# A causal attention and routed experts kernel: k held in both partition halves and split where it lies, q alone stacked

## The chip, the cores and the metric

The kernel runs on one core of one Trainium2 chip. The metric is the device time of one execution in microseconds (us). Before the change three runs took 506.85, 504.80 and 505.87 us; their median is 505.87 us. Inside the core five engines run their own instruction streams: TensorE (PE, with its weight loads shown apart as PEld), VectorE (DVE), ScalarE (ACT), GpSimd (POOL), and SyncE (SP), which here issues most of the transfers. They wait for one another by semaphores.

## The reference

Four batches, 12 heads each, 448 positions, head size 64, float32. Causal attention gives rows of 768 numbers; each of the 1792 rows then goes to one of 8 experts (the best of 8 logits), and the result is weighted by the gate's probability.

```python
scores = (q @ k.T) / sqrt(64);  scores[above the diagonal] = -1e9
attn = exp(scores - max);  attn /= sum(attn) + 1e-9
x = (attn @ v)                       # 4 x 12 x 448 x 64, laid out as 1792 x 768
logits = x @ w_gate + modality_bias[modality_id]
e_idx = argmax(logits);  gate_w = softmax(logits)[e_idx]
out = gate_w * (relu(x @ w1[e_idx]) @ w2[e_idx])      # w1 768x1024, w2 1024x768
```

## The kernel before

**Products in two parts.** A float32 number is split into a part that TensorE takes in its faster 32-bit format (hi) and the rest (lo); a product is then made of hi·hi, lo·hi and hi·lo. For the scores of a head the contraction is only 64 long, so two of the products share one matmul: hi of q lies in partitions 0 to 63 and lo of q in 64 to 127, and k's hi lies in both halves. That is "stacking".

**The attention loop** is one software pipeline over 48 heads, `iteration(n)` at L1070. In iteration n the scores of head n are made on PE (L269) and reduced on DVE (L278, which also copies them out as `p`), head n-1 gets its exp on ACT (L288), head n-2 is transposed on PE (L300) and split into `ph` on ACT (L318) and `pl` on DVE (L319), head n-3 is multiplied with v on PE (L332, L339), and head n-4 is added up on DVE (L363). Every four heads end in L392, where the rows come back to token order on PE, in L410 and L420, where they are normalised on DVE (a quarter of them on POOL) into `row`, and, every twelve heads, in a store of `row` to `xs` by SP (L432). `row` has four buffers, so a row of the next batch waits until the store of the one four before it has landed.

**The heads come in pairs.** Pair m holds heads 2m and 2m+1. `load_qk(m)` (L189, SP) brings q and k of both heads, 128 partitions, 448 KB, at the end of iteration 2m-6. `split_qk(m)` on POOL (iteration 2m-4) makes hi of q and k (L194, 128x896) and lo of q (L195, 128x448). `stack_qk(m)` (start of iteration 2m-3) issues four transfers on SP (L211, L212), 64 partitions by 896 numbers each, so that `st` holds (hi, lo) of q one above the other and hi of k twice. `split_kl(m)` on POOL at the end of iteration 2m-3 makes lo of k (L200) and two copies of q, `qz`, each with the other head's half zeroed (L202, twice). Product one is `st` of q by `st` of k, product two is `qz` by lo of k. The first three pairs go a direct way without a split (`first_load`, L225). There are two buffers of `raw` and `hl` and three sets of the stacked tiles.

**What stands around it.** POOL also splits v of the next four heads (L242, L247), and, from head 45 on, the first expert's weights (L671, L672). The routing of batches 0 to 2 is done beside the attention of later heads. Thus the expert of the first block of tokens is known before attention ends: `start_w1` (L663) loads its weights, `pre_ids` (L716) reads its token numbers from tables in DRAM, and `fetch_x` gathers its rows (DVE L726 and L727, POOL L728). `later(n, f)` queues f behind the scores of iteration n, `before(n, f)` behind those but ahead of the split, and the lists on each engine are strictly in order of the code. Twelve small tiles that the routing needs (`tcol`, `evals`, `cth`, `gt64`, `eq1`, `ctri`, `e8`, `e8v`, `ebase`, `ebneg`) are made on DVE in iterations 1 to 4, from integers that POOL writes with iota in the setup. The experts' blocks follow from about 215 us to the end.

Of the kernel before, what the change touches and what calls it, by code (L numbers as in the profile page):

```python
# [21 lines left out]
def attention_moe(  # L22
# [14 lines left out]
    A = nc.scalar  # L37
    B, HP, _, _, S = qk.shape
    H = 2 * HP
# [38 lines left out]
    def cst(name, shape, dt=F32):  # L78
        return const.tile(shape, dt, name=name)
# [59 lines left out]
    def row():  # L139
        return early.tile([128, DM], F32, tag="row", name="row", bufs=4)  # L140
# [30 lines left out]
    qz = [stack_view(w1h[KA - 2]), *(atp.tile([128, 2, S], F32R, name=f"qz{j}") for j in range(2))]  # L171
    kl = [t.rearrange("p k c -> p (k c)")[:, j * S:(j + 1) * S] for t, j in ((xh, 0), (xl, 0), (xh, 1))]
    praw = [
# [9 lines left out]
    def ots(gr, j):  # L183
        return ut[gr % 2][:, j]

    def load_qk(m):
        b, j = divmod(m, H // 2)
        raw[m] = t = R([128, 2, S], F32, "raw")
        nc.sync.dma_start(out=t, in_=qk[b, j])  # L189

    def split_qk(m):
        x = raw[m]
        hl = R([128, 3, S], F32R, "hl")
        P.tensor_scalar(out=hl[:, 1:3], in0=x, scalar1=1.0, scalar2=0.0, op0=ALU.mult, op1=ALU.add)  # L194
        P.tensor_tensor(out=hl[:, 0], in0=x[:, 0], in1=hl[:, 1].bitcast(F32), op=ALU.subtract)  # L195
        hls[m] = hl

    def split_kl(m):
        x, hl = raw.pop(m), hls.pop(m)
        P.tensor_tensor(out=kl[m % 3], in0=x[:, 1], in1=hl[:, 2].bitcast(F32), op=ALU.subtract)  # L200
        for a in range(2):
            P.tensor_scalar(  # L202
                out=qz[m % 3][:, a], in0=x[:, 0], scalar1=half[:, a:a + 1], scalar2=0.0, op0=ALU.mult, op1=ALU.add
            )

    def stack_qk(m):
        hl, st = hls[m], stk[m % 3]
        u, d = slice(0, 64), slice(64, 128)
        src = hl.bitcast(F32)
# [6 lines left out]
    stk = [[stack_view(t[KA - 1]) for t in (w1h, w1l)]]  # L216
    for j in range(2):
        t = prp.tile([128, 2, 2, S], F32R, name=f"st{j}", bufs=1)
        stk.append([t[:, a] for a in range(2)])

    def first_view(m, c):
        k = 3 * m + c
        return raw1[k % K1][:, k // K1 * S:k // K1 * S + S]

    def first_load(m):  # L225
        nc.sync.dma_start(out=first_view(m, 2), in_=qk[0, m, :, 1])
        for a in range(2):
            r = slice(a * 64, a * 64 + 64)
            nc.sync.dma_start(out=first_view(m, a)[r], in_=qk[0, m, r, 0])
            spl[2 * m + a] = (first_view(m, a), first_view(m, 2), None, None)  # L230
# [642 lines left out]
    with tc.manual_schedule():  # L873
# [25 lines left out]
        make_identity(nc, ident)  # L899
        P.tensor_copy(ident2[:, 128:192], ident[:, 0:64])  # L900
        P.memset(wi, 0.0)
        P.memset(sums, 1.0)
        V.memset(vraw[64:128, 3, :], 0.0)
        for a in range(2):
            for j in range(2):
                V.memset(half[j * 64:j * 64 + 64, a:a + 1], float(a == j))
        for s in range(3):
            eng = P if s else V
            eng.memset(praw[s][0], 0.0)
            eng.memset(praw[s][1][:, 192:256], 0.0)  # L910
            eng.memset(praw[s][2][:, 320:384], 0.0)
            eng.memset(praw[s][3][:, 448:512], 0.0)
        wg = w_gate.rearrange("(j a p) e -> a p j e", a=2, p=64)
        for a in range(2):
# [50 lines left out]
        def cast(o, x):  # L965
            return lambda: V.tensor_copy(o, x)

        def times_gt(o, x, y):
            return lambda: V.scalar_tensor_tensor(out=o, in0=x, scalar=0.0, in1=y, op0=ALU.is_gt, op1=ALU.mult)

        def fma(o, x, mul, add):
            return lambda: V.tensor_scalar(out=o, in0=x, scalar1=mul, scalar2=add, op0=ALU.mult, op1=ALU.add)

        def cmp(o, x, y, op):
            return lambda: V.tensor_scalar(out=o, in0=x, scalar1=y, scalar2=None, op0=op)

        setup = [
            (1, cast(tcol, ti)), (1, cast(evals, itmp)), (1, cast(cth, cthi)), (2, cast(gt64, tji)),
            (2, cmp(eq1, dti, -1, ALU.is_equal)), (3, times_gt(gt64, dti, gt64)),
            (3, cmp(ctri, ctri_i, 0, ALU.is_gt)), (3, fma(e8, evals, -1.0, float(E))),  # L980
            (4, cast(e8v, e8)), (4, lambda: V.memset(e8v[64:128, 0], 0.0)),
            (4, fma(ebase, evals[:, 0, :], float(NT), 0.0)), (4, fma(ebneg, ebase, 1.0, -float(EMPTY))),
        ]

# [20 lines left out]
        e0 = []  # L1005
        W1AT = (11, 12, 13, 14, 15, 15)

# [53 lines left out]
        for k in range(KA):  # L1061
            later(NHEAD - KA + k, lambda k=k: w1_chunk(k, P))
        for n, f in setup:
            later(n, f)
        later(4, setup_4)
# [346 lines left out]
```

## Time and profile before

| | |
|---|---|
| profiled execution | 504.5 us, span 502.8 us |
| runs timed | 504.80, 505.87, 506.85 us |
| PE, PEld | busy 476.4 us (95%), 441.9 us (88%) |
| DVE, ACT, POOL | 295.9 us (59%), 276.7 us (55%), 239.2 us (48%) |
| q and k pairs loaded (`raw<-in_qk_dram`) | 21 transfers of 448 KB |
| stacks (`st<-hl`, `w1h<-hl`, `w1l<-hl`) | 56 + 14 + 14 transfers of 224 KB |

The share of busy time is that of the whole execution; in single stretches other engines are as full as PE. A row of the timeline gives start, duration, engine, line, operation, output from input, shape and count, and in square brackets the engine's idle time before it and what ended that.

### The profile page before, as it was taken

Reading aid. Unit: us, or ns where it says so; the run is one execution under the profiler, and the core shown is the slowest. Engines: PE = TensorE matmul, PEld = TensorE weight load, DVE = VectorE, ACT = ScalarE, POOL = GpSimd, SP = SyncE. Lnnn points to the kernel's source line nnn. Section 1 sums busy time; section 2 is a strip of 40 time slices with the busy share of each in tenths; the row PEclk is TensorE's granted clock in tenths of the full one; section 3 lists DMA queues with packets and bytes.
Section 4 is the critical chain, followed back from the end, with each engine's and each line's share of the span. In section 5 each row is a group of like instructions: output and inputs, shape, how many; then the busy total and the mean of one; then the engine's idle time right before and its main releaser. Section 6 shows DMA issues by size and latency. Waiting matters only on the chain.

```text
span 502.8 us, 10244 instructions
## 1 busy us (share of the span) xinstructions
PE 476.4 (95%) x3311; PEld 441.9 (88%) x3311; DVE 295.9 (59%) x874; ACT 276.7 (55%) x680; POOL 239.2 (48%) x313
## 2 busy tenths in 40 slices
PE   8899999999998987999999999999999999999990
PEld 6589999999987986878999999999999999888770
DVE  6999999999989967887512016442111120183490
ACT  5689999999997965616222216432121211383670
POOL 7899999899999898660311102202001000021131
PEclk9999999999999988999999999999999999999996
DMA  6998799997988689473496302863101001076300
GB/s 183 207 238 214 198 234 281 235 224 208 263 207 215 106 224 350 141 130 64 98 349 256 96 25 83 299 248 90 41 1 53 33 2 63 33 273 188 108 14 6
DMA packets 43817, 78.92 MB, mean 157 GB/s; under 512 B 15582, under 2 KB 27614, under 8 KB 43744
## 3 DMA queue, kind: packets, MB, share of 16 engines
q1 hardware_dynamic: 40704, 67.06, 49.4%
q0 software_dynamic: 3040, 11.03, 6.4%
q8 instruction: 28, 0.46, 0.4%
q14 instruction: 45, 0.37, 0.3%
HBM read 48.10 MB, written 11.89 MB: 119 GB/s over the span
## 4 chain that ended last, share of the span: by engine, by line
PE 67%; DVE 11%; DMA 6%; POOL 5%; issue 3%; ACT 3%; SPq 1%; DVEq 0%; POOLq 0%; ACTq 0%
PE g L749 7%; PE g L747 7%; PE g L748 7%; PE pt L300 5%; PE sa L269 3%; PE x L392 3%; PE ot L339 3%; PE ot L332 3%; PE sb L269 3%; DVE p L278 2%; DVE pl L319 2%; PE ot L749 2%; PE ot L748 2%; PE x L749 2%; PE x L748 2%
## 5 line engine op out<-in xcount | busy, mean ns | idle before, releaser
L728 POOL DMA_INDIRECT xg<-xs,idg x18 | 20.8, 1154 | 159.0 <-DVEq L1322 79.9
L288 ACT ACTIVATE p<-p,nm 128x448 f32<-128x448 f32 x192 | 94.8, 497 | 2.8 <-DVE nm L278 2.8
L766 DVE SCALAR_TENSOR_TENSOR htl<-g,hth 128x256 fp32r<-128x256 f32 x40 | 16.7, 424 | 104.6 <-ACT hth L765 104.6
L747 PE MATMUL g<-xh,w1h 128*128 128x256 f32 x240 | 67.1, 279 | 0.4 <-DVE htl L766 0.4
L749 PE MATMUL g<-xh,w1l 128*128 128x256 f32 x240 | 67.2, 280 | 0.0
L748 PE MATMUL g<-xl,w1h 128*128 128x256 f32 x240 | 67.0, 279 | 0.0
L319 DVE TENSOR_TENSOR pl<-pt,ph 128x1024 fp32r<-128x1024 f32 x48 | 58.4, 1218 | 5.7 <-ACT ph L318 5.3
L300 PE MATMUL pt<-ident,p 128*128 128x128 f32 x480 | 61.0, 275 | 0.0
L332 PE MATMUL ot<-ph,vhl 128*128 128x448 f32 x192 | 50.8, 305 | 7.8 <-DVE ut L363 7.3
L300 PEld LDWEIGHTS pt<-ident,p 128*128 128x128 f32 x480 | 55.9, 142 | 1.3 <-issue 0.2
L318 ACT ACTIVATE ph<-pt 128x1024 fp32r<-128x1024 f32 x48 | 49.1, 1024 | 10.1 <-PE pt L300 8.4
L765 ACT ACTIVATE hth<-g 128x256 fp32r<-128x256 f32 x40 | 15.1, 382 | 63.5 <-PE g L749 60.5
L747 PEld LDWEIGHTS g<-xh,w1h 128*128 128x128 f32 x240 | 44.9, 187 | 0.6 <-DVE htl L766 0.6
L748 PEld LDWEIGHTS g<-xl,w1h 128*128 128x128 f32 x240 | 45.1, 188 | 0.0
L749 PEld LDWEIGHTS g<-xh,w1l 128*128 128x128 f32 x240 | 45.1, 188 | 0.0
L807 POOL DMA_INDIRECT out_dram<-row,idg x14 | 16.4, 1175 | 59.7 <-ACTq L1306 33.5
L332 PEld LDWEIGHTS ot<-ph,vhl 128*128 128x128 f32 x192 | 33.6, 194 | 10.1 <-DVE ut L363 8.4
L278 DVE CUSTOM_DVE_ANT_0 p<-sa,mask 128x448 f32<-128x448 f32 x96 | 36.1, 412 | 3.3 <-PE sa L269 3.0
L288 ACT ACTIVATION_READ_ACCUMULATOR p<-p,nm 128x1 f32 x192 | 36.4, 190 | 0.0
L278 DVE CUSTOM_DVE_ANT_0 p<-sb,mask 128x192 f32<-128x192 f32 x96 | 36.3, 411 | 0.0
L339 PE MATMUL ot<-pl,vhl 128*64 128x64 f32 x192 | 35.5, 300 | 0.6 <-DVE pl L319 0.6
L357 ACT ACTIVATE hol<-ot 64x448 f32<-64x448 f32 x48 | 26.0, 542 | 16.7 <-PE ot L332 13.5
(360 smaller groups left out, 1303.1 us busy)
## 6 DMA issues: line engine op xcount, KB each, us to landing
st<-hl SPq DMA_DIRECT2D x56, 224.0 KB
raw<-in_moe_w_dram SPq DMA_DIRECT2D x24, 512.0 KB
raw<-in_qk_dram SPq DMA_DIRECT2D x21, 448.0 KB
raw<-in_moe_w_dram SPq DMA_DIRECT2D x20, 384.0 KB
vraw<-in_v_dram SPq DMA_DIRECT2D x12, 384.0 KB
xs<-row SPq DMA_DIRECT2D x12, 384.0 KB
w1h<-hl SPq DMA_DIRECT2D x14, 224.0 KB
w1l<-hl SPq DMA_DIRECT2D x14, 224.0 KB
```

Source lines behind the costliest of these rows:

```text
L269: nc.tensor.matmul(outs[i], lhsT=a[:, q0:q0 + n], rhs=z[:, :w], start=(last == 0), stop=(last == 1 or qh is None))
L278: V.tensor_tensor_reduce(out=z, in0=o, in1=m, scale=-scale, scalar=3.0e38, op0=ALU.add, op1=ALU.min, accum_out=nm[:n, i:i + 1],)
L288: A.activation(out=z, in_=z, func=AF.Exp, bias=nm[:n, i:i + 1], scale=-1.0, accum_out=sums[:n, b, i, h:h + 1],)
L300: nc.tensor.transpose(out=o, in_=a, identity=i)
L318: A.activation(out=ph, in_=t, func=AF.Copy)
L319: V.tensor_tensor(out=pl, in0=t, in1=ph.bitcast(F32), op=ALU.subtract)
L332: nc.tensor.matmul(o[:, q0:S], lhsT=t[:rows, kt, h].rearrange("p a d -> p (a d)"), rhs=ph[:rows, c0:c1], start=(n == 0), stop=(n == 1),)
L339: nc.tensor.matmul(o[0:D, q0:S], lhsT=t[:rows, kt, h, 0], rhs=pl[:rows, c0:c1], start=False, stop=False)
L357: A.activation(out=t, in_=ov[g][64:128, :S], func=AF.Copy)
L747: nc.tensor.matmul(o, lhsT=ah, rhs=bh, start=first, stop=False)
L748: nc.tensor.matmul(o, lhsT=ah, rhs=bl, start=False, stop=False)
L749: nc.tensor.matmul(o, lhsT=al, rhs=bh, start=False, stop=last)
```

## The change

Pair m is now loaded as q once (128x448) and k twice, with both heads of k side by side, once into partitions 0 to 63 and once into 64 to 127 (64x896 each): 672 KB and three transfers for 448 KB and one. `split_q` makes hi and lo of q (128x448 each). `split_k` makes hi and lo of k at full width (128x896 each), where k lies, straight into the tiles that PE reads (`kk`). `stack_q` has four transfers of 64x448 numbers, 112 KB each. Product two now takes the same stacked q as product one. The masked copies of q and their mask `half` are gone. The numbers of matmuls and of bytes loaded for the first three pairs stay; their k comes in two transfers for one, of which the first pair's second goes out from ACT.

Apart from that the twelve routing tiles are made in the setup, ahead of DVE's first reduction, and POOL's iotas ahead of its memset of `wi`; the two memsets of `xg` go from DVE (iterations 2 and 3) to POOL (iteration 0); `pre_ids` goes from iterations 42 and 43 to 43 and 44, `fetch_x` from behind the scores of 44 and 45 to ahead of the splits of 45 and 46, and the first two weight loads fall into one iteration.

```diff
     def load_qk(m):
-        raw[m] = t = R([128, 2, S], F32, "raw")
-        nc.sync.dma_start(out=t, in_=qk[b, j])
-
-    def split_qk(m):
-        hl = R([128, 3, S], F32R, "hl")
-        P.tensor_scalar(out=hl[:, 1:3], in0=x, scalar1=1.0, scalar2=0.0, op0=ALU.mult, op1=ALU.add)
-        P.tensor_tensor(out=hl[:, 0], in0=x[:, 0], in1=hl[:, 1].bitcast(F32), op=ALU.subtract)
+        raw[m] = t = R([128, 3, S], F32, "raw")
+        nc.sync.dma_start(out=t[:, 0], in_=q_rows(m))
+        for r in (slice(0, 64), slice(64, 128)):
+            nc.sync.dma_start(out=t[r, 1:3], in_=k_rows(m))
+
+    def split_q(m):
+        x = raw[m][:, 0]
+        hl = R([128, 2, S], F32R, "hl")
+        P.tensor_scalar(out=hl[:, 1], in0=x, scalar1=1.0, scalar2=0.0, op0=ALU.mult, op1=ALU.add)
+        P.tensor_tensor(out=hl[:, 0], in0=x, in1=hl[:, 1].bitcast(F32), op=ALU.subtract)
 
-    def split_kl(m):
-        P.tensor_tensor(out=kl[m % 3], in0=x[:, 1], in1=hl[:, 2].bitcast(F32), op=ALU.subtract)
+    def split_k(m):
+        x, (kh, kl) = raw.pop(m)[:, 1:3], kk[m % 3]
+        P.tensor_scalar(out=kh, in0=x, scalar1=1.0, scalar2=0.0, op0=ALU.mult, op1=ALU.add)
+        P.tensor_tensor(out=kl, in0=x, in1=kh.bitcast(F32), op=ALU.subtract)
         for a in range(2):
-            P.tensor_scalar(
-                out=qz[m % 3][:, a], in0=x[:, 0], scalar1=half[:, a:a + 1], scalar2=0.0, op0=ALU.mult, op1=ALU.add
-            )
-
-    def stack_qk(m):
-        for a, r in enumerate((u, d)):
-            nc.sync.dma_start(out=st[a][u].bitcast(F32), in_=src[r, 1:3])
-            nc.sync.dma_start(out=st[a][d].bitcast(F32), in_=src[r, 0:3:2])
+            spl[2 * m + a] = (qs[m % 3][:, a], kh[:, a], qs[m % 3][:, a], kl[:, a])
+
+    def stack_q(m):
+        src = hls.pop(m).bitcast(F32)
         for a in range(2):
-            spl[2 * m + a] = (st[a][:, 0], st[a][:, 1], qz[m % 3][:, a], kl[m % 3])
+            r = slice(a * 64, a * 64 + 64)
+            for u in range(2):
+                nc.sync.dma_start(out=qs[m % 3][u * 64:u * 64 + 64, a].bitcast(F32), in_=src[r, 1 - u])
...
+        V.tensor_copy(tcol, ti)
+        V.tensor_copy(evals, itmp)
+        V.tensor_copy(cth, cthi)
...
         for j in range(2):
-            later(2 + j, lambda j=j: V.memset(xg[j], 0.0))
+            later(0, lambda j=j: P.memset(xg[j], 0.0))
...
-        W1AT = (11, 12, 13, 14, 15, 15)
+        W1AT = (12, 12, 13, 14, 15, 15)
...
                 for t in range(NPRE):
-                    later(n + 11 + t, lambda t=t: pre_ids(t))
-                    later(n + 13 + t, lambda t=t: fetch_x(0, 2 * S, t))
+                    later(n + 12 + t, lambda t=t: pre_ids(t))
+                    before(n + 14 + t, lambda t=t: fetch_x(0, 2 * S, t))
```

POOL's order for two neighbouring pairs in the middle of the attention, before (`vhl` is v's split, `by_shift` and `slot` belong to the routing, `xh` and `qz_155` are lo of k and the masked q):

```order
L194 TENSOR_SCALAR hl<-raw 128x896
L195 TENSOR_TENSOR hl<-raw,hl 128x448
L242 TENSOR_SCALAR vhl<-vraw 128x16x64
L247 TENSOR_TENSOR vhl<-vraw,vhl 128x16x64
L540 TENSOR_SCALAR slot<-by_shift_98 128x1
L552 TENSOR_SCALAR by_shift_98<-by_shift_98,slot 128x1
L200 TENSOR_TENSOR xh<-raw,hl 128x448
L202 TENSOR_SCALAR qz_155<-raw,half 128x448 x2
```

The same place on POOL in the changed kernel (`kk_167` is hi and lo of k):

```order
L201 TENSOR_SCALAR hl<-raw 128x448
L202 TENSOR_TENSOR hl<-raw,hl 128x448
L245 TENSOR_SCALAR vhl<-vraw 128x16x64
L250 TENSOR_TENSOR vhl<-vraw,vhl 128x16x64
L543 TENSOR_SCALAR slot<-by_shift_98 128x1
L555 TENSOR_SCALAR by_shift_98<-by_shift_98,slot 128x1
L207 TENSOR_SCALAR kk_167<-raw 128x896
L208 TENSOR_TENSOR kk_167<-raw,kk_167 128x896
```

Nothing changes its place; the first half of the work shrinks in width and the second grows, and what `L200` and `L202` did in three instructions is done in two wider ones.

SP's order at the end of the attention, before (`st_170` is the stack of the last pair, `idq` the token numbers, `raw_116` to `raw_118` the first expert's weights, `xs` a row's store):

```order
L663 DMA raw_116<-in_moe_w_dram 128x1024
L432 DMA xs<-row 128x768
L211 DMA st_170<-hl 64x896
L212 DMA st_170<-hl 64x2x448
L211 DMA st_170<-hl 64x896
L212 DMA st_170<-hl 64x2x448
L680 TENSOR_LOAD sch_110
L716 ISA
L716 DMA idq<-table_70 128x2
```

The same place on SP in the changed kernel (`xl` is where the last pair's stacked q goes):

```order
L217 DMA xh<-hl 64x448 x4
L435 DMA xs<-row 64x768
L435 DMA xs<-row 128x768
L217 DMA xl<-hl 64x448 x4
L683 TENSOR_LOAD sch_109
L719 ISA
L719 DMA idq<-table_70 128x2
```

Three more reads of `idq` on, SP's order in the changed kernel goes on (`raw_115` and `raw_116` are the weights):

```order
L719 DMA idq<-table_73 128x2
L683 TENSOR_LOAD sch_109
L666 ISA
L666 DMA raw_115<-in_moe_w_dram 128x1024
L666 ISA
L666 DMA raw_116<-in_moe_w_dram 128x1024
L435 DMA xs<-row 128x768
```

The first four reads of `idq` and the first weight load have gone from ahead of the last stack to behind it. The second row store has come ahead of that load, and the third now stands right behind two loads in a row; the second four reads of `idq` follow that store instead of going ahead of it.

## Rows read from the trace of the kernel before

**Rows 1.** Windows: stretch, length, busy of PE, PEld, DVE, ACT, POOL, clock, DMA, GB/s.
```profile
36.00:66.00 30.00, 30.00 (x243) 28.56 (x241) 28.59 (x96) 29.08 (x84) 28.39 (x43) 1.00 0.83 211
...
180.00:195.00 15.00, 11.53 (x76) 10.67 (x75) 9.74 (x36) 8.32 (x22) 12.85 (x16) 0.84 0.87 271
...
196.00:203.00 7.00, 7.00 (x57) 6.25 (x57) 6.90 (x20) 6.08 (x21) 6.83 (x7) 0.94 0.94 338
```

**Rows 2.** Timeline of PE, the first 28 us: start, us, instruction, idle before and releaser.
```profile
16.99 0.47 PE L339 MATMUL ot<-pl,vhl 128*64 128x64 f32 x2 [0.61 <-DVE pl L319]
...
22.76 0.56 PE L332 MATMUL ot<-ph,vhl 128*128 128x448 f32 x2 [1.66 <-DVE ut L363]
...
27.59 0.56 PE L332 MATMUL ot<-ph,vhl 128*128 128x448 f32 x2 [0.40 <-DVE ut L363]
```

**Rows 3.** Timeline of DVE, the first 26 us.
```profile
6.60 0.62 DVE L278 CUSTOM_DVE_ANT_0 p<-sa,mask 128x448 f32<-128x448 f32 x1 [1.96 <-PE sa L269]
...
10.84 0.15 DVE L966 CAST tcol<-row 128x1 f32<-128x1 int32 x1
10.91 1.61 DVE L966 CAST evals<-row 128x32 f32<-128x32 int32 x1
...
24.90 0.87 DVE L972 TENSOR_SCALAR ebneg<-ebase 128x8 f32<-128x8 f32 x1
```

**Rows 4.** Timeline of POOL, the first 16 us.
```profile
10.12 2.36 POOL L247 TENSOR_TENSOR vhl<-vraw,vhl 128x1024 fp32r<-128x1024 f32 x1
13.52 0.95 POOL L194 TENSOR_SCALAR hl<-raw 128x896 fp32r<-128x896 f32 x1 [1.04 <-DMA raw<-in_qk_dram]
14.55 1.13 POOL L195 TENSOR_TENSOR hl<-raw,hl 128x448 fp32r<-128x448 f32 x1
```

**Rows 5.** Instructions by line and shape on POOL: count, busy us, mean ns, idle before.
```profile
L195 POOL TENSOR_TENSOR hl<-raw,hl 128x448 fp32r<-128x448 f32 x21 | 24.1, 1147 | 1.7
L194 POOL TENSOR_SCALAR hl<-raw 128x896 fp32r<-128x896 f32 x21 | 19.9, 949 | 3.5 <-DMA raw<-in_qk_dram 2.7 <-DMA w1l<-hl 0.5
L202 POOL TENSOR_SCALAR qz<-raw,half 128x448 fp32r<-128x448 f32 x28 | 17.6, 642 | 0.0
```

**Rows 6.** Timeline of POOL, later: a wait in the routing, then the last pair.
```profile
91.37 0.24 POOL L467 TENSOR_TENSOR eq<-eq,m 128x32 f32<-128x32 f32 x1 [1.89 <-DVE m L463]
...
177.10 1.13 POOL L195 TENSOR_TENSOR hl<-raw,hl 128x448 fp32r<-128x448 f32 x1
...
184.20 1.27 POOL L202 TENSOR_SCALAR qz<-raw,half 128x448 fp32r<-128x448 f32 x2
185.79 1.11 POOL L728 DMA_INDIRECT xg<-xs,idg  x1
```

**Rows 7.** Timeline of PE, heads 44 and 46.
```profile
178.29 0.44 PE L269 MATMUL sa<-st 128*128 128x448 f32 x1 [2.75 <-DMA st<-hl]
...
187.16 0.46 PE L269 MATMUL sa<-st 128*128 128x448 f32 x1
```

**Rows 8.** Timeline of DVE, the reduction of head 46 and its waits.
```profile
190.45 0.16 DVE L726 TENSOR_REDUCE idg<-idq 128x1 int32<-128x4 int32 x1 [3.24 <-DMA idq<-table]
...
194.29 0.42 DVE L420 TENSOR_TENSOR row<-x,rec 128x256 f32<-128x256 f32 x1 [1.33 <-DMA xs<-row]
194.73 0.62 DVE L278 CUSTOM_DVE_ANT_0 p<-sa,mask 128x448 f32<-128x448 f32 x1
```

**Rows 9.** Timeline of SP's issues in the same stretch.
```profile
180.20 0.49 SPq L211 DMA_DIRECT2D st<-hl  x1
...
184.18 3.08 SPq L716 DMA_DIRECT2D idq<-table  x4
187.46 0.33 SPq L663 DMA_DIRECT2D raw<-in_moe_w_dram  x1
187.89 0.38 SPq L432 DMA_DIRECT2D xs<-row  x1
```

**Rows 10.** Chain of waits: start, us, what; the stretch before head 44.
```profile
170.57 7.59 DMA st<-hl
```

More of the change, by code (lines that the diff above doesn't have):

```diff
@@ L37, in attention_moe @@
     A = nc.scalar
-    B, HP, _, _, S = qk.shape
+    B, HP, _, _, _, S = qk.shape
     H = 2 * HP
@@ L169, in stack_view @@
         return t[:, 0:2 * S].rearrange("p (c s) -> p c s", c=2)
-    qz = [stack_view(w1h[KA - 2]), *(atp.tile([128, 2, S], F32R, name=f"qz{j}") for j in range(2))]
-    kl = [t.rearrange("p k c -> p (k c)")[:, j * S:(j + 1) * S] for t, j in ((xh, 0), (xl, 0), (xh, 1))]
+    qs = [stack_view(t) for t in (w1h[KA - 2], *(x.rearrange("p k c -> p (k c)") for x in (xh, xl)))]
     praw = [
@@ L216, in attention_moe @@
-    stk = [[stack_view(t[KA - 1]) for t in (w1h, w1l)]]
+            r = slice(a * 64, a * 64 + 64)
+            for u in range(2):
+                nc.sync.dma_start(out=qs[m % 3][u * 64:u * 64 + 64, a].bitcast(F32), in_=src[r, 1 - u])
+    kk = [[stack_view(t[KA - 1]) for t in (w1h, w1l)]]
     for j in range(2):
-        t = prp.tile([128, 2, 2, S], F32R, name=f"st{j}", bufs=1)
-        stk.append([t[:, a] for a in range(2)])
+        t = prp.tile([128, 2, 2, S], F32R, name=f"kk{j}", bufs=1)
+        kk.append([t[:, a] for a in range(2)])
@@ L225, in first_load @@
     def first_load(m):
-        nc.sync.dma_start(out=first_view(m, 2), in_=qk[0, m, :, 1])
         for a in range(2):
             r = slice(a * 64, a * 64 + 64)
-            nc.sync.dma_start(out=first_view(m, a)[r], in_=qk[0, m, r, 0])
+            (nc.sync if m or not a else nc.scalar).dma_start(out=first_view(m, 2)[r], in_=k_rows(m)[:, a])
+            nc.sync.dma_start(out=first_view(m, a)[r], in_=q_rows(m)[r])
             spl[2 * m + a] = (first_view(m, a), first_view(m, 2), None, None)
@@ L903, in attention_moe @@
         V.memset(vraw[64:128, 3, :], 0.0)
-        for a in range(2):
-            for j in range(2):
-                V.memset(half[j * 64:j * 64 + 64, a:a + 1], float(a == j))
         for s in range(3):
@@ L912, in attention_moe @@
             eng.memset(praw[s][3][:, 448:512], 0.0)
+        V.tensor_copy(tcol, ti)
+        V.tensor_copy(evals, itmp)
+        V.tensor_copy(cth, cthi)
+        V.tensor_copy(gt64, tji)
+        V.tensor_scalar(out=eq1, in0=dti, scalar1=-1, scalar2=None, op0=ALU.is_equal)
+        V.scalar_tensor_tensor(out=gt64, in0=dti, scalar=0.0, in1=gt64, op0=ALU.is_gt, op1=ALU.mult)
+        V.tensor_scalar(out=ctri, in0=ctri_i, scalar1=0, scalar2=None, op0=ALU.is_gt)
+        V.tensor_scalar(out=e8, in0=evals, scalar1=-1.0, scalar2=float(E), op0=ALU.mult, op1=ALU.add)
+        V.tensor_copy(e8v, e8)
+        V.memset(e8v[64:128, 0], 0.0)
+        V.tensor_scalar(out=ebase, in0=evals[:, 0, :], scalar1=float(NT), scalar2=0.0, op0=ALU.mult, op1=ALU.add)
+        V.tensor_scalar(out=ebneg, in0=ebase, scalar1=1.0, scalar2=-float(EMPTY), op0=ALU.mult, op1=ALU.add)
         wg = w_gate.rearrange("(j a p) e -> a p j e", a=2, p=64)
@@ L960, in attention_moe @@
         for j in range(2):
-            later(2 + j, lambda j=j: V.memset(xg[j], 0.0))
+            later(0, lambda j=j: P.memset(xg[j], 0.0))
             later(1 + j, lambda j=j: V.memset(sls[j][64:128, 0, E:E + 1], 1.0e6))
             later(1 + j, lambda j=j: V.memset(lts[j][64:128, 0], 0.0))
[L965 to L983, printed above, removed]
         def setup_4():
@@ L1062, in attention_moe @@
             later(NHEAD - KA + k, lambda k=k: w1_chunk(k, P))
-        for n, f in setup:
-            later(n, f)
         later(4, setup_4)
@@ L1388 @@
         if name == "qk":
-            a = _np.stack([inputs["q"], inputs["k"]], axis=2)
-            b, h, _, s, d = a.shape
-            a = a.reshape(b, h // 2, 2, 2, s, d).transpose(0, 1, 2, 5, 3, 4).reshape(b, h // 2, 2 * d, 2, s)
+            b, h, s, d = a.shape
+            p, r = (inputs[x].reshape(b, h // 2, 2, s, d) for x in "qk")
+            p = p.transpose(0, 1, 2, 4, 3).reshape(b, h // 2, d, 2, s)
+            a = _np.stack([p, r.transpose(0, 1, 4, 2, 3)], axis=2)
         elif name == "v":
```

43 lines of the change are left out of this document (21 added, 22 removed).

## The prediction

> **What bounds the kernel now.** I read the windows first, then what PE waited for. In the middle of the attention, 36 to 66 us [rows 1], PE is busy for all 30 us at full clock, but POOL is close behind it: 28.39 of 30 us. So a few tenths more on POOL for each pair of heads will not fit; they have to pile up as lateness. From 180 to 195 us PE is busy for 11.53 of 15 us at a mean clock of 0.84: here 3.47 us of PE are lost, and the DMA engines are 0.87 busy. From 196 to 203 us PE is full again. Three places therefore decide: the start, POOL's lead over PE, and the end of the attention, about 165 to 200 us. Behind that the experts' stage runs on the same code, and I cost it at nothing; it starts later or earlier as the attention ends.
>
> **The start.** PE stood still for 0.61, 1.66 and 0.40 us because DVE was late [rows 2], 2.67 us. DVE was late because of the constants and memsets put among the heads: the twelve constants, from the first at 10.84 to the last at 24.90 us [rows 3], took 6.6 us together, far more than so small tiles need. The cast of `evals` shows why: 32 numbers a partition took 1.61 us and ended at 12.52 us, just when POOL's subtraction ended, 10.12 + 2.36 = 12.48 us [rows 4]. In the change they run ahead of the first reduction. DVE had idled 1.96 us there before 6.60 us [rows 3], and POOL then has only memsets and iotas of some tenths each. Bounds: twelve times 0.15 us (the first, which no POOL instruction held up) is 1.8 us and fits in the idle time; 6.6 us as they ran would put the first reduction off by 4.6 us and eat the whole gain. POOL's long subtraction is not near, so I go by the short end: the first reduction 0.4 us later, a gain of 2.67 - 0.4 = 2.3 us.
>
> [...]
>
> **POOL's work per pair.** Before: 0.949 + 1.147 + 1.147 (lo of k has the shape of lo of q) + 2 x 0.642 = 4.53 us [rows 5]. After: hi of q at the width of one masked copy, 0.64; lo of q, 1.147; hi of k over 896 numbers like the old first one, 0.949; and a subtraction over 896 numbers, which no row shows. Upper bound: two over 448, 2.29. Lower: v's subtraction over 1024 numbers took 2.36 us [rows 4], of which 896/1024 is 2.07. I take 2.10, nearest to the row for one instruction. That is 4.84 us, and as the second pair of instructions now also waits for its first (the gap between the end at 13.52 + 0.95 = 14.47 and 14.55 us, 0.08 us [rows 4]), 4.92. So 0.39 us more per pair, and for 21 pairs 8.2 us (at 2.29, 12.2; without the gap and at 2.07, 5.9).
>
> To that comes the start: POOL waited 1.04 us for the first pair [rows 4], and each pair now brings 224 KB more (672 for 448). At the rate of the middle stretch, 211 / 0.83 = 254 GB/s [rows 1], that is 0.9 us per pair. Before pair 3 it delays POOL by about that. Later loads are issued iterations ahead and are hidden, or take up what the stacks leave: these fall from 896 to 448 KB, so that a pair moves 1120 KB for 1344. Against it stands POOL's own idle time, which lateness uses up first: 1.89 us in the routing [rows 6], and 1.7 of the 2.7 us that L194 waited for its input [rows 5] (the rest is the 1.04 above), 3.6 us. So POOL is 8.2 + 0.9 - 3.6 = 5.5 us late at the last pair, which ended at 184.20 + 1.27 = 185.5 us [rows 6], and now at 191.0 us.
>
> **What PE makes of it.** Head 46, the first of that pair, began at 187.16 us [rows 7], 1.7 us after the split. Thus 191.0 us is late for PE by 3.8 us, and the 2.3 us won at the start are used up on the way: a PE that runs ahead only waits for the split. The same for head 44's wait of 2.75 us [rows 7], for a stack under way for 7.59 us [rows 10]: half the bytes shorten the transfer, but the split ahead of it comes some 5 us later. At head 46 the lateness does not all reach the end, because head 46 did not go through at 187.16 us. Its reduction ran only at 194.73 us [rows 8], behind a row of the normalisation at 194.29 us, which waited for the store of an older row, and before that DVE stood 3.24 us for `idq` (190.45 us). So the true gate is in SP's order.
>
> **SP at the end of the attention.** Before, the last stack went out at 180.20 us, then four reads of `idq` (3.08 us), the second weight load at 187.46 and the third row store at 187.89 us [rows 9]. After: the last stack waits for its q. Before, that q was done at 177.10 + 1.13 = 178.2 us, and k began at 185.5 - 1.27 - 1.147 = 183.1 us [rows 5, 6]; the 4.9 us of other work between them stay. So from 191.0 us back by k's 0.949 + 2.10 = 3.05 us and by 4.9 us, q is done at 183.1 us, and SP, which issued the stack at 180.20 us before, waits for it. Four issues at 0.49 us [rows 9] end at 185.1 us, 0.9 us behind the old first read of `idq` at 184.18 us; if the four take as long as before, 3.98 us from the first to that read, it is 2.9 us. I take 1.5 us, nearer the short end, since each carries half the bytes. Then the store has the four reads and one more load of 512 KB ahead of it: at 338 / 0.94 = 360 GB/s [rows 1] 1.46 us. In its favour the gather of 384 KB of rows (185.79 us [rows 6]) now stands behind it, 1.1 us at the same rate. Sum: 1.5 + 1.46 - 1.1 = 1.9 us. The second four reads follow the store on SP instead of preceding it, and the wait of DVE for them (3.24 us [rows 8]) moves behind that row with them; for what they disturb there I add 0.1 us. The reduction of head 46 then is at 194.73 + 2.0 = 196.7 us. POOL's k at 191.0 us is ahead of it, and PE's clock at the time is not the limit.
>
> **Forecast.** 504.5 + 2.0 = 506.5 us for a profiled execution. The median of the runs is 505.87, 1.4 us above the profiled execution, so 507.9 us is what I predict.
>
> **Rivals.**
> *POOL becomes the bound.* The subtraction is at its upper end, 2.29 us, so that the pairs cost 12.2 us instead of 8.2, and k of the last pair is done at 195.0 us. Its q, and with it the last stack, the reads of `idq`, the weights and the store behind it on SP's list, come 4.0 us later than in the forecast. DVE had idled 1.33 us before the row at 194.29 us [rows 8], which takes up that much: 2.0 + 4.0 - 1.3 = +4.7 us, 510.6 us. It decides once k of the last pair ends after 191.0 + 1.3 = 192.3 us. For it: POOL's 28.39 of 30 us [rows 1]. Against it: no wait of PE in these rows names POOL [rows 2, 7].
> *The gain is kept.* POOL's idle time between the routing steps is larger than two rows show, so that it stays ahead; the 2.3 us of the start and the 2.75 us at head 44 remain, less 1 us for the store behind two loads: -4.0 us, 501.9 us. For it: 224 KB less a pair, and DVE freed of 6.6 us of constants. Against it: the sums above of rows that differ only in width.
> [...]
>
> [...]
>
> **How the numbers follow.** Forecast 0.45, POOL as the bound 0.25, the gain kept 0.25, others 0.05. About 0.5%, 2.5 us, is what a measurement of this kernel can tell from no change. The forecast's own range is 506 to 510 us: two thirds of its chance lie within 2.5 us of 505.87, the rest above. With the rival that is slower: slower 0.15 + 0.25 + 0.02 = 0.42; faster 0.25; same 0.30 + 0.03 = 0.33. The range reaches to both rivals: 501.5, just under the kept gain, to 512.5, above the bound by POOL.
>
> **What would show it.** Right: no wait of PE for `pl` or `ut` in the first 28 us; the 896-wide subtraction at 2.07 to 2.29 us; k of the last pair done near 191 us; the reduction of head 46 near 196.7 us behind a row that waits for `xs`. Wrong: PE waiting for `kk` from about head 20 on (the bound by POOL), or head 44 without a wait and head 46's reduction before 194 us (the gain kept). If the first reduction comes after 8 us, the constants were mis-sized.

## The result and the profile after

Six runs of the changed kernel took 508.02 to 510.00 us, median 509.36; six of the kernel before, on the same chip, 504.80 to 507.27, median 505.89. The ratio is 1.007, with a 95% interval of 1.0046 to 1.0093: slower by 3.5 us, or 0.7%. The forecast was 507.9 us, only 2.0 us above before, in a range of 501.5 to 512.5, with slower as the likeliest of the three outcomes.

The profiled execution of after took 510.0 us (span 507.9) and is the slowest of its six; that of before, 504.5 us (span 502.8), lies just under the fastest of its own six. Between the two traces therefore lie 5.1 us of span, of which the medians bear out 3.5; a difference of 1 us between two traces alone says little.

**The start.** First PE's one long wait in the timeline, then PE's window behind it, DVE's first 10 us and POOL's start (start, us, instruction, idle before and releaser; the window has the columns of [rows 1]).

```profile
9.83 1.86 PE L272 MATMUL sa<-raw,raw 128*128 128x448 f32 x2 [2.15 <-DVE nm L281]
```
```profile
10.00:16.00 6.00, 6.00 (x18) 4.12 (x19) 2.19 (x14) 4.00 (x16) 4.45 (x4) 0.50 0.69 162
```
```profile
4.14 2.00 DVE L926 CAST evals<-row 128x32 f32<-128x32 int32 x1
...
7.44 1.46 DVE L935 TENSOR_SCALAR ebase<-evals 128x8 f32<-128x8 f32 x1
...
9.01 0.62 DVE L281 CUSTOM_DVE_ANT_0 p<-sa,mask 128x448 f32<-128x448 f32 x1
```
```profile
4.14 0.82 POOL L916 MEMSET wi<- 128x864 f32 x1
...
7.46 1.42 POOL L973 MEMSET xg<- 128x768 f32 x2
...
14.75 0.57 POOL L201 TENSOR_SCALAR hl<-raw 128x448 fp32r<-128x448 f32 x1 [1.39 <-DMA raw<-in_qk_dram]
...
18.99 1.05 POOL L245 TENSOR_SCALAR vhl<-vraw 128x1024 fp32r<-128x1024 f32 x1 [2.46 <-DMA vraw<-in_v_dram]
...
23.51 2.10 POOL L208 TENSOR_TENSOR w1l<-raw,w1h 128x896 fp32r<-128x896 f32 x1
```

The three waits of [rows 2] are gone, and one of 2.15 us stands in their place. Behind that wait PE's granted clock stood at 0.50 from 10 to 16 us; there the kernel before had 1.00 and got through 35 matmul instructions where the changed one got through 18. The first reduction runs at 9.01 us instead of 6.60 [rows 3]: the cast of 32 numbers holds DVE from 4.14 to 6.14 us while POOL's memsets follow one another without a gap, and `ebase` (8 numbers) ends at 8.90 us, just after the memsets of `xg` at 8.88 us. Head 12 thus starts at 53.19 us instead of 51.17. On POOL the first split starts 1.2 us later than in [rows 4], and the second split of v waits 2.46 us for its load. So k of pair 3 is done at 23.51 + 2.10 = 25.6 us. In the kernel before it was at 20.90 + 1.28 = 22.2 us, by this row of its timeline:

```profile
20.90 1.28 POOL L202 TENSOR_SCALAR w1h<-raw,half 128x448 fp32r<-128x448 f32 x2
```

**POOL's work per pair**, from the instructions by line and shape (count, busy us, mean ns, idle before):

```profile
L208 POOL TENSOR_TENSOR kk<-raw,kk 128x896 fp32r<-128x896 f32 x14 | 29.6, 2112 | 1.2
...
L202 POOL TENSOR_TENSOR hl<-raw,hl 128x448 fp32r<-128x448 f32 x21 | 24.2, 1150 | 1.8
...
L207 POOL TENSOR_SCALAR kk<-raw 128x896 fp32r<-128x896 f32 x14 | 13.2, 944 | 0.0
...
L201 POOL TENSOR_SCALAR hl<-raw 128x448 fp32r<-128x448 f32 x21 | 12.1, 576 | 1.8 <-DMA raw<-in_qk_dram 1.4 <-issue 0.2
```

0.576 + 1.150 + 0.944 + 2.112 = 4.78 us, with the gap of 0.08 us between the two halves 4.86, against 4.53 before [rows 5].

**The end of the attention.** The windows that answer to [rows 1], then POOL, PE, DVE and SP.

```profile
36.00:66.00 30.00, 29.71 (x237) 27.95 (x236) 28.73 (x95) 28.88 (x82) 28.23 (x37) 1.00 0.64 165
180.00:195.00 15.00, 13.48 (x106) 12.22 (x105) 13.12 (x43) 12.86 (x39) 13.00 (x16) 1.00 0.69 190
196.00:203.00 7.00, 4.16 (x21) 3.44 (x22) 3.79 (x15) 3.54 (x11) 5.47 (x6) 0.83 0.98 339
```
```profile
182.66 0.57 POOL L201 TENSOR_SCALAR hl<-raw 128x448 fp32r<-128x448 f32 x1 [0.18 <-issue]
...
190.35 2.10 POOL L208 TENSOR_TENSOR kk<-raw,kk 128x896 fp32r<-128x896 f32 x1
```
```profile
176.13 0.47 PE L272 MATMUL sa<-w1l,w1h 128*128 128x448 f32 x1 [1.55 <-POOL w1l L208]
...
192.78 0.65 PE L272 MATMUL sa<-kk,xl 128*128 128x448 f32 x2
```
```profile
197.54 0.42 DVE L423 TENSOR_TENSOR row<-x,rec 128x256 f32<-128x256 f32 x1 [1.68 <-DMA xs<-row]
199.60 0.16 DVE L729 TENSOR_REDUCE idg<-idq 128x1 int32<-128x4 int32 x1 [1.64 <-DMA idq<-table]
...
199.84 0.61 DVE L281 CUSTOM_DVE_ANT_0 p<-sa,mask 128x448 f32<-128x448 f32 x1
```
```profile
176.10 0.33 SPq L194 DMA_DIRECT2D raw<-in_qk_dram  x1
...
183.25 2.97 SPq L217 DMA_DIRECT2D xl<-hl  x4
187.33 2.96 SPq L719 DMA_DIRECT2D idq<-table  x4
190.84 0.87 SPq L666 DMA_DIRECT2D raw<-in_moe_w_dram  x2
191.80 0.38 SPq L435 DMA_DIRECT2D xs<-row  x1
```

The DMA share in the middle fell from 0.83 to 0.64, so the transfers did get fewer; PE lost nearly nothing there, and won nothing either. The last pair is done at 190.35 + 2.10 = 192.45 us (185.47 before), head 46 starts at 192.78 (187.16 [rows 7]), and its reduction runs at 199.84 us (194.73 [rows 8]): 5.1 us later, just the difference of the two spans. From there to the end it is 308.1 us in both (502.8 - 194.73 and 507.9 - 199.84), so between these two traces the rest neither adds nor gives back. Of PE's waits only one names POOL's split, at head 42; head 46 finds it busy with other work until 192.78 us. The loss has moved in time, too: PE's poor stretch was 180 to 195 us, and now is 196 to 203 us, with 4.16 of 7 us.

### The profile page after: what moved, and what is told of

The parts are those of the page before. It is cut to its first block, busy times and chain, and to the rows that moved or that the text cites. A ratio compares the mean times of both kernels' runs of the same rounds, so it can differ in the third digit from the quotient of the medians.

```text
span 507.9 us, 10322 instructions
## 1 busy us (share of the span) xinstructions
PE 479.6 (94%) x3311; PEld 443.2 (87%) x3311; DVE 294.2 (58%) x868; ACT 277.2 (55%) x680; POOL 246.8 (49%) x294
## 4 chain that ended last, share of the span: by engine, by line
PE 66%; DVE 10%; DMA 7%; POOL 7%; issue 5%; ACT 2%; SPq 1%; DVEq 0%; POOLq 0%; ACTq 0%
PE g L750 7%; PE g L751 7%; PE g L752 7%; PE pt L303 6%; PE sa L272 4%; PE sb L272 4%; PE ot L342 3%; PE ot L335 3%; PE x L395 2%; PE ot L752 2%; DMA idq<-table 2%; PE ot L751 2%; PE x L752 2%; PE x L751 2%; PE x L750 2%
## 5 line engine op out<-in xcount | busy, mean ns | idle before, releaser
L303 PE MATMUL pt<-ident,p 128*128 128x128 f32 x480 | 62.1, 278 | 0.0
L303 PEld LDWEIGHTS pt<-ident,p 128*128 128x128 f32 x480 | 57.3, 145 | 1.6 <-issue 0.7
L342 PE MATMUL ot<-pl,vhl 128*64 128x64 f32 x192 | 34.3, 293 | 0.0
L395 PE MATMUL x<-wi,ut 128*128 128x144 f32 (+1 forms) x180 | 30.7, 293 | 3.4 <-DVE row L423 3.4
```

Source lines behind the costliest of these rows:

```text
L303: nc.tensor.transpose(out=o, in_=a, identity=i)
L342: nc.tensor.matmul(o[0:D, q0:S], lhsT=t[:rows, kt, h, 0], rhs=pl[:rows, c0:c1], start=False, stop=False)
L395: nc.tensor.matmul(x[:n, j * 2 * XW:(j + 1) * 2 * XW], lhsT=ots(gr, j)[:, q0:q0 + n], rhs=wi[:, u * (GH // 2) + j].rearrange("p a c -> p ( ...
```

## Experiments

All were run with several rounds beside the kernel before. "k last" is when POOL has finished the last pair, "head 46" when its reduction on DVE starts, both from the timeline of the run's profile. The runs were made in several sets, in which the kernel before had medians of 503.5 to 505.9 us; so runs of different sets are compared by their ratios.

| run | k last, us | head 46, us | span, us | median, us | ratio to before (95%) |
|---|---|---|---|---|---|
| before | 185.5 | 194.73 | 502.8 | 505.89 | 1 |
| changed | 192.5 | 199.84 | 507.9 | 509.36 | 1.0070 (1.0046 to 1.0093) |
| e1_qk_only | 192.8 | 199.95 | 507.9 | 510.26 | 1.0100 (1.0074 to 1.0126) |
| e2_const_only | 185.7 | 194.02 | 503.1 | 504.57 | 0.9995 (0.9975 to 1.0015) |
| e3_sched_only | 184.5 | 193.12 | 504.3 | 505.80 | 1.0010 (0.9985 to 1.0034) |
| e4_old_const | 192.7 | 200.08 | 508.6 | 510.07 | 1.0089 (1.0057 to 1.0121) |
| e5_half_lo | 180.5 | 188.46 | 499.0 | 498.25 | 0.9870 (0.9838 to 0.9902) |
| e6_raw3 | 191.4 | 196.97 | 503.8 | 506.81 | 1.0063 (1.0039 to 1.0086) |
| e7_load34 | 185.5 | 194.15 | 502.9 | 504.88 | 1.0021 (1.0003 to 1.0039) |
| e8_pool_const | 184.6 | 194.15 | 503.4 | 505.25 | 1.0030 (1.0012 to 1.0049) |
| e9_no_mask | 211.9 | | 531.6 | 533.29 | 1.0578 (1.0550 to 1.0605) |
| e10_swap | 179.5 | 189.17 | 496.1 | 499.83 | 0.9930 (0.9904 to 0.9955) |
| e11_swap_rest | 177.6 | 187.57 | 494.0 | 501.02 | 0.9958 (0.9936 to 0.9980) |
| e12_k_act | 191.8 | 197.86 | 506.3 | 509.74 | 1.0107 (1.0083 to 1.0130) |

**From head 46 to the end.** Head 46 is a mark, not the end. In the thirteen profiles that have it in the table, 306.4 (e11) to 311.2 us (e3) pass from its reduction to the end of the span. These two differ in PE's granted clock behind head 46: 0.50 in the window below in e3, 1.00 in e11 (columns of [rows 1], e3 first):

```profile
194.00:202.00 8.00, 8.00 (x37) 6.85 (x37) 6.46 (x19) 3.82 (x13) 7.80 (x7) 0.50 0.70 235
```
```profile
194.00:202.00 8.00, 7.29 (x57) 6.66 (x56) 6.76 (x11) 4.81 (x13) 7.76 (x7) 1.00 0.68 232
```

So 1 to 3 us won or lost at head 46 in one profile need not show in the time.

**Which of the three parts costs.** The change was taken apart: loads, splits and stacks of q and k alone (e1); constants, iotas and memsets alone (e2); the order at the end of the attention alone (e3); and the whole change with the constants back (e4).

e1_qk_only and e4_old_const, edits to the changed kernel (e1 has the old schedule as well):

```diff
-        V.tensor_copy(tcol, ti)
...
+        for n, f in setup:
+            later(n, f)
...
-        W1AT = (12, 12, 13, 14, 15, 15)
+        W1AT = (11, 12, 13, 14, 15, 15)
```

> The loads, splits and stacks of q and k as changed; constants and schedule as before. Theory 1 (the start counts): the first reduction is back near 6.6 us and head 12 near 51 us, POOL's work per pair still grows by 0.39 us, k of the last pair is done near 190 us instead of 192.5, and the median lies 1 to 3 us above before. Theory 2 (POOL's work per pair sets the end and swallows the start): k of the last pair stays near 192 us and the median at 3 to 4 us above before.

> The changed kernel with the constants, iotas and memsets of xg back at their old places. Theory 1: 2 us below the changed kernel, about 507.4 us. Theory 2: the same as the changed kernel within 0.7 us, since POOL's lateness sets the end.

e2_const_only and e3_sched_only put the other two parts into the kernel before:

```diff
+        V.tensor_copy(tcol, ti)
...
-        for n, f in setup:
-            later(n, f)
```

> Only the twelve constants, the iotas and the two memsets of xg moved; the rest as before. Theory 1 (the start counts): the first reduction comes near 9.0 us instead of 6.6, head 12 about 2 us later than before, and the end 1 to 2 us later (part of it lost in the wait at head 44, 2.75 us in the kernel before). Theory 2 (swallowed): head 12 late too, but the end within 0.5 us of before.

```diff
-                    later(n + 11 + t, lambda t=t: pre_ids(t))
-                    later(n + 13 + t, lambda t=t: fetch_x(0, 2 * S, t))
+                    later(n + 12 + t, lambda t=t: pre_ids(t))
+                    before(n + 14 + t, lambda t=t: fetch_x(0, 2 * S, t))
```

> Only the reads of the token numbers, the gather and the first weight load moved; the rest as before. Theory 3 (the order at the end of the attention costs): the third row store behind two weight loads lands about 1.5 us later, the reduction of head 46 runs near 196 us instead of 194.7, and the median is 1 to 2 us above before. Rival: the last stack goes out earlier, as it has less ahead of it, and the median is 0 to 2 us below before.

The part on q and k costs the whole of it: 1.0100 alone, 0.9995 and 1.0010 for the others. Alone it even costs 5 us, above the 3 to 4 us of theory 2, and e4 with 1.0089 is not within 0.7 us of the changed kernel's 1.0070; the intervals of the three meet, so this difference stays open. Theory 1, which wanted both below the changed kernel, falls, and theory 2 stands in the main: k of the last pair is at 192.5 to 192.8 us whether or not the constants are early. In e2 the first reduction is late just as in the changed kernel, and head 12 starts at 51.81 us instead of 51.17, a third of the 2 us expected; nothing of it reaches the end. In e1, where PE starts on time, PE runs into POOL as early as head 10:

```profile
43.84 0.47 PE L272 MATMUL sa<-kk,xl 128*128 128x448 f32 x1 [1.42 <-POOL kk L208]
...
61.37 0.47 PE L272 MATMUL sa<-kk,xh 128*128 128x448 f32 x1 [1.69 <-POOL kk L208]
```

The late start of the changed kernel thus hides waits for POOL that come into view without it. Theory 3 was missed too: in e3 head 46 is 1.6 us earlier, and the end is the same; its rival, 0 to 2 us below before, isn't borne out either (1.0010).

**Is it POOL's work, or the loads and SP's order?** e5 makes lo of k half as wide; e6 gives raw q and k a third buffer.

```diff
-        P.tensor_tensor(out=kl, in0=x, in1=kh.bitcast(F32), op=ALU.subtract)
+        P.tensor_tensor(out=kl[:, 0], in0=x[:, 0], in1=kh[:, 0].bitcast(F32), op=ALU.subtract)
-            spl[2 * m + a] = (qs[m % 3][:, a], kh[:, a], qs[m % 3][:, a], kl[:, a])
+            spl[2 * m + a] = (qs[m % 3][:, a], kh[:, a], qs[m % 3][:, a], kl[:, 0])
```

> The changed kernel with lo of k made for the first head of a pair only, 448 numbers instead of 896 (the second head uses the first one's, so its scores lack their own correction). POOL's work per pair falls by 0.96 us, and nothing else changes. If POOL's work per pair is the cause: k of the last pair is done 6 us or more earlier, before 187 us, and the median falls by 3 to 5 us to near that of before. If the loads or the order on SP are the cause: k at most 2 us earlier, since POOL then waits for its loads, and the median falls by less than 1.5 us.

```diff
-        raw[m] = t = R([128, 3, S], F32, "raw")
+        raw[m] = t = prp.tile([128, 3, S], F32, tag="raw", name="raw", bufs=3)
```

> The changed kernel with three buffers of raw q and k instead of two, so that a load on SP no longer waits until POOL has split the pair two before, and the stores and stacks behind it on SP's list don't wait either. If POOL's late splits pass to the end through SP's list: no wait of PE near 135 us for a row (2.4 us), the last load issued near 170 us instead of 176, and the median 1.5 to 3 us lower. If POOL's work alone is the bound: k of the last pair within 1 us of 192.5 us, and the median within 0.7 us of the changed kernel.

e5 is the strongest result. Its subtraction and its window in the middle:

```profile
L208 POOL TENSOR_TENSOR kk<-raw,kk 128x448 fp32r<-128x448 f32 x14 | 16.1, 1148 | 1.2
```
```profile
36.00:66.00 30.00, 30.00 (x243) 28.56 (x242) 28.98 (x97) 29.17 (x83) 27.25 (x40) 1.00 0.73 189
```

With 2.112 - 1.148 = 0.96 us less per pair k of the last pair is done 12 us earlier, and the median goes from 3.5 us above before to 5.6 below. More than was expected, and below the kernel before, whose POOL had also been late. e6 does move the last load from 176.10 to 170.20 us, as expected of it, but k last comes only 1.1 us earlier and the ratio, 1.0063, can't be told from that of the change: the load that waits for its buffer was in the main a sign of POOL's lateness and not a way by which it reached the end. Nor did PE's wait near 135 us go: at 137.35 us it is 2.32 us, behind a DVE that had waited 2.07 us for POOL. Head 46 is 2.9 us earlier in its profile; the medians don't show it.

**Why POOL starts late.** e7 loads 224 KB more with pairs 3 and 4 of the kernel before; e12 lets ACT issue the second k transfer of each of the first three pairs, and puts their two q transfers behind both of k.

```diff
+    EXTRA = (3, 4)
+    more = cxt
...
         nc.sync.dma_start(out=t, in_=qk[b, j])
+        if m in EXTRA:
+            nc.sync.dma_start(out=more[:, 0:S], in_=qk[b, j, :, 1])
```

> The kernel before with 224 KB more loaded with each of the first two split pairs, into a tile that nobody reads; work on POOL as before. If the bytes explain the late start of POOL's splits: k of pair 3 is done at 24 to 25.5 us instead of 22.2 (25.6 in the changed kernel), but the lead comes back through POOL's idle time, and the median is 0 to 1 us above before. If the start is late for another reason: pair 3 within 1 us of 22.2 us.

```diff
-            (nc.sync if m or not a else nc.scalar).dma_start(out=first_view(m, 2)[r], in_=k_rows(m)[:, a])
+            (nc.scalar if a else nc.sync).dma_start(out=first_view(m, 2)[r], in_=k_rows(m)[:, a])
+        for a in range(2):
+            r = slice(a * 64, a * 64 + 64)
             nc.sync.dma_start(out=first_view(m, a)[r], in_=q_rows(m)[r])
```

> The changed kernel with the second k transfer of all of the first three pairs issued by ACT, not only that of the first pair, so that SP issues two transfers of 0.64 us fewer ahead of pair 3. If POOL's late start comes from SP's longer list of issues: pair 3's first load issued near 10.5 us instead of 11.8 (9.8 before), k of pair 3 done near 24.5 us instead of 25.6, and the median up to 1 us lower. If not: pair 3 within 0.5 us of 25.6 us.

In e7 k of pair 3 is done at 22.5 us (22.2 before): as bytes alone, queued behind the pair's load, they explain 0.3 of 3.4 us. In e12 SP reaches pair 3's load a microsecond earlier than the changed kernel (11.78 us there, 9.77 before), and k of pair 3 is at 22.81 + 2.10 = 24.9 us instead of 25.6:

```profile
10.76 0.61 SPq L194 DMA_DIRECT2D raw<-in_qk_dram  x1
```
```profile
22.81 2.10 POOL L208 TENSOR_TENSOR w1l<-raw,w1h 128x896 fp32r<-128x896 f32 x1
```

So SP's number of issues is a part, some 0.7 us. The rest lies at the second split of v, which waits in e12 too (2.08 us for its load, 2.46 in the changed kernel, 0.64 in the kernel before); why that load comes late stays open, with three transfers ahead of it where one stood. For k itself POOL did not wait: the 21 splits of L207 have no idle time before them. At the end e12 won nothing, where up to 1 us had been set: 1.0107, k last 191.8 us.

**Is a gain at the start swallowed?** e8 takes the kernel before and makes the constants on POOL.

```diff
+        P.tensor_copy(tcol, ti)
+        P.tensor_copy(evals, itmp)
...
-        for n, f in setup:
-            later(n, f)
```

> The kernel before with the twelve constants made on POOL at the end of its setup instead of on DVE among the heads (one of them in two instructions instead of one). PE's waits in the first 28 us fall from 2.7 us to under 1 us. If what is won at the start is swallowed by POOL and the end of the attention: median within 0.7 us of before. If a gain at the start is kept: 2 us lower.

PE's waits of the start are gone but for 0.25 us, and it waits for POOL instead, where the kernel before has no wait:

```profile
57.22 0.47 PE L269 MATMUL sa<-xl,qz 128*128 128x448 f32 x1 [1.56 <-POOL qz L202]
```

The end is 1.0030, 1.4 us above before where 0.7 had been set: swallowed, and a little more. Why more isn't shown: POOL, which now makes the constants, is done with the last pair 0.9 us earlier than before, and head 46 is 0.6 us earlier.

**Less work on POOL in the kernel before.** e9 and e10 start from the kernel before and drop the masked copies. e9 takes 64 partitions for product two; e10 keeps 128, turns the second head's stack upside down, and lets lo of q meet the other head's lo of k. e11 is e10 with the constants and the schedule of the change.

```diff
-            P.tensor_scalar(
-                out=qz[m % 3][:, a], in0=x[:, 0], scalar1=half[:, a:a + 1], scalar2=0.0, op0=ALU.mult, op1=ALU.add
-            )
+            spl[2 * m + a] = (*spl[2 * m + a], hl[r, 1], kl[m % 3][r])
```

> The kernel before without the two masked copies of q per pair: product two takes hi of q where it was split and lo of k, 64 partitions of each, with hl in three buffers instead of two. POOL's work per pair falls from 4.53 to 3.25 us, the matmuls keep their columns and number, the loads and stacks stay as before. If POOL's work per pair sets the end of the attention also in the kernel before: k of the last pair done 4 to 6 us earlier (near 180 us instead of 185.5) and the median 3 to 5 us below before, near that of the kernel with half of k's lo. If the gain there came from the changed loads and stacks: less than 1 us below before.

```diff
-            nc.sync.dma_start(out=st[a][u].bitcast(F32), in_=src[r, 1:3])
-            nc.sync.dma_start(out=st[a][d].bitcast(F32), in_=src[r, 0:3:2])
+            nc.sync.dma_start(out=st[a][r].bitcast(F32), in_=src[r, 1:3])
+            nc.sync.dma_start(out=st[a][(d, u)[a]].bitcast(F32), in_=src[r, 0:3:2])
-            spl[2 * m + a] = (st[a][:, 0], st[a][:, 1], qz[m % 3][:, a], kl[m % 3])
+            spl[2 * m + a] = (st[a][:, 0], st[a][:, 1], st[a][:, 0], kl[m % 3])
```

> The kernel before without the masked copies, all matmuls over 128 partitions: the second head of a pair is stacked upside down (lo of q above hi), and product two takes the stacked q by the tile that holds lo of k of both heads, so that hi of q meets its own lo of k; the other half of that product is lo by lo of the wrong head, a size of rounding. POOL's work per pair falls by 1.28 us, nothing is added. If POOL's work per pair sets the end of the attention: k of the last pair done at 179 to 182 us instead of 185.5, the median 3 to 6 us below before. If the last run's loss was from another cause than the 64 partitions: slower than before here too.

> The same, with the constants, iotas, memsets and the order at the end of the attention as in the changed kernel. If these two count for nothing while POOL is late, but cost or gain once it isn't: 1 to 2 us away from the kernel with the heads upside down alone (later by the start, 2 us; earlier by the schedule); if they count for nothing: within 0.7 us of it.

e9 is far off both theories, 29 us slower: it lost on PE what it won on POOL. Between 36 and 66 us PE is full, as before, but with 193 matmul instructions for 243, and POOL has 9 us to spare:

```profile
36.00:66.00 30.00, 30.00 (x193) 23.53 (x193) 23.14 (x80) 22.39 (x66) 21.03 (x33) 1.00 0.67 179
```

The weight loads show what differs. In e9, where 128 and 64 partitions alternate, and in the kernel before at the same place of a head:

```profile
53.24 0.18 PEld L266 LDWEIGHTS sa<-xh,hl 64*128 64x128 f32 x1 [0.22 <-issue]
53.63 0.19 PEld L266 LDWEIGHTS sb<-st 128*128 128x128 f32 x1 [0.21 <-issue]
```
```profile
51.28 0.19 PEld L269 LDWEIGHTS sa<-xh,w1h 128*128 128x128 f32 x1
51.49 0.19 PEld L269 LDWEIGHTS sb<-w1h 128*128 128x128 f32 x1
```

At these two changes between 64 and 128 rows the weights were loaded only 0.2 us after the load before had ended, in the same instant as the matmul started (53.24 and 53.63 us on PE, too); in the kernel before the load at 51.28 us is ahead of its matmul at 51.49. The scores of a head took 2.1 us (52.85 to 54.97) instead of 1.2 (51.17 to 52.35).

e10 has the gain that was expected: 0.9930, 3.7 us below before, a version faster than both kernels.

```profile
36.00:66.00 30.00, 30.00 (x244) 28.70 (x243) 28.97 (x99) 29.13 (x83) 24.01 (x35) 1.00 0.84 215
```
```profile
188.73 0.42 DVE L414 TENSOR_TENSOR row<-x,rec 128x256 f32<-128x256 f32 x1 [1.18 <-DMA xs<-row]
189.17 0.61 DVE L272 CUSTOM_DVE_ANT_0 p<-sa,mask 128x448 f32<-128x448 f32 x1
```

POOL has 6 of 30 us to spare in the middle, and head 46 is reduced 5.6 us earlier than before, still behind a row that waits for a store: the gate at the end is the same, only earlier. So the loss of e9 does come with its 64 partitions, and not from leaving out the copies. e11 wins nothing more (0.9958; its profile is the fastest of its twelve runs, 496.0 to 504.1 us). Its median lies about 1 us above e10's, and the intervals meet: whether the constants and the schedule count once POOL is early isn't settled.

## Why the prediction was right, and where its terms were not

**The cause: shown. The way: read from the trace.** That POOL's work per pair sets the time is shown from both sides: e5 took work off POOL in the changed kernel and got the time back, e10 did the same in the kernel before, with loads and stacks of the same number and size. The way to head 46 that was forecast, through SP, is what the timeline shows: POOL's hi of q is done at 182.66 + 0.57 = 183.23 us, SP issues the last stack at 183.25 and behind it the reads of `idq`, the weights and the third row store, at 191.80 us instead of 187.89. No run tests this way by itself: the row that this store takes was done on DVE only at 191.26 + 0.41 = 191.67 us, so a store free of SP's list would hardly have gone earlier.

**The number: in part luck.** The result lay between the forecast (+2.0 us) and the rival "POOL becomes the bound" (+4.7). The rival's threshold was passed, with k last at 192.45 us against 192.3, but not for the rival's reason: the subtraction took 2.112 us and not 2.29. Nor did its sign come, PE waiting for `kk` from head 20 on; there is one such wait, at head 42. Two of the forecast's own four signs missed: k last was to be near 191 us, and head 46 near 196.7. The range of 11 us took in faster, same and slower, so that the time lies in it says little; and the terms below err both ways.

**POOL per pair: right.** The wide subtraction was taken at 2.10 and took 2.112 us. Hi of q is 0.576 and not 0.64, so a pair costs 4.86 - 4.53 = 0.33 us more, not 0.39; 21 pairs give 6.9 us instead of 8.2. From pair 3 to the last the lateness grew from 3.4 to 7.0 us, 3.6 us, where 20 pairs add 6.6: 3.0 us went into POOL's idle time, 3.6 had been forecast.

**POOL's start: mis-sized.** Put at 0.9 us, the time of 224 KB; pair 3 was 3.4 us late, of which 0.33 is its own work. The bytes alone were the wrong measure, as e7 shows; SP's longer list of issues is some 0.7 us (e12); the rest is open. The sum for k last was 191.0 us, against 192.45. How much of the end this error of 2 us costs isn't shown: e12 took back 0.7 us of it, at pair 3 and at k last alike, and the time did not fall.

**The constants: mis-sized, and the clock left out.** Of the bounds 0 and 4.6 us for the first reduction 0.4 was taken; it was 9.01 - 6.60 = 2.4, past the 8 us that the prediction itself had named as the sign of it. "POOL then has only memsets and iotas of some tenths each" was the step that failed: they stand back to back, and one cast lasted over eleven of them, from 4.14 to 6.14 us. In e1, where only the splits of v are near, it took 0.31 us and ended at 11.14 us, as POOL's instruction of that time ended at 11.10:

```profile
10.83 0.31 DVE L966 CAST evals<-row 128x32 f32<-128x32 int32 x1
```
```profile
10.05 1.05 POOL L245 TENSOR_SCALAR vhl<-vraw 128x1024 fp32r<-128x1024 f32 x1 [2.64 <-DMA vraw<-in_v_dram]
```

In the changed kernel the cast's end, too, came just after that of one of POOL's memsets, 5.91 + 0.20 = 6.11 us; that POOL held up the casts is read from these ends alone, and by what is not shown. The sum also had no term for PE's clock, which stood at 0.50 for 6 us behind the wait. Instead of a gain of 2.3 us head 12 started 2.0 us late. That a gain of the start would be swallowed was right (e8), and a loss there was, too (e1, e2, e4): that is why this error cost nothing.

**SP at the end: half right.** The last stack was forecast at 183.1 us and went out at 183.25, by luck: all of q was to be done by then and was so only at 183.31 + 1.14 = 184.45 us, but the first transfer needs only hi of q. Its four issues took 2.97 us and not four times 0.49, so the reads of `idq` began 187.33 - 184.18 = 3.15 us later, where 1.5 was taken. The row behind the store was to come about 1.9 us later and came 197.54 - 194.29 = 3.25 later. And the second read of `idq` was given 0.1 us, as a wait that moves "behind that row". It did, but ahead of head 46's reduction: 199.84 - 197.54 - 0.42 = 1.9 us between the two. The text ahead of the prediction says that `before(n, f)` puts f behind the scores of iteration n; that is wrong. It runs ahead of them, so `fetch_x` stands ahead of the reduction on DVE. 2.0 us forecast for head 46 became 5.1. Still, with the old schedule (e1) head 46 is at 199.95 us: the lateness reaches it in either order.

**The other rival.** The gain was not kept: POOL was 7.0 us late at the last pair, head 44 waited 1.35 us and head 46's reduction ran after 194 us. That the loads of k, 64 partitions each, made POOL late is not borne out at k's splits, which never waited for them (0.0 us of idle time before L207); POOL's wait for pair 3's load grew from 1.04 to 1.39 us; whether they held up v's load is open.

## What to carry to other kernels

A helper engine as full as POOL here, 95% (28.39 of 30 us) beside a PE at 100%, is a bound in waiting: the price of a change on it was not the 0.33 us of one pair but that of 20 pairs, 6.6 us, less the 3.0 us that went into idle time, and a gain of the bounding engine ahead of it was lost again (e8, 1.0030). Ask first what can be left out there: e10, which makes no masked copies and moves the same bytes as before, gained 3.7 us, where the change, with fewer bytes, lost 3.5. And a wait that is moved in an in-order list has to be followed to the instruction that it now stands ahead of, in the order itself, not in the name of the queue.

## What the runs showed of the hardware that was not expected

In e9, 29 us slower in all, matmuls over 64 partitions between such over 128 cost more than full ones: the scores of a head took 2.1 us (52.85 to 54.97) instead of 1.2 at the same columns, and five of their eight weight loads began no earlier than their matmuls. On VectorE a cast of 32 numbers took 2.00 us beside GpSimd's memsets in a row, and 0.31 us in e1. And a wait of PE cost more than its length: after one of 2.15 us, in the changed kernel, the granted clock stood at 0.50 from 10 to 16 us, and PE got through 18 matmul instructions instead of 35.
